# The first attention unit of a gated-linear-attention and expert-MLP kernel, written out by itself with 64x64 score tiles

## The chip, the cores and the metric

The kernel runs on one core of one Trainium2 chip. The metric is the device time of one execution in microseconds (us); the time of a kernel is the median of its runs. PE (TensorE) multiplies, DVE (VectorE) and ACT (ScalarE) do elementwise work, POOL (GpSimd) clears and copies, SP (SyncE) issues loads. PSUM is where products arrive; the other tiles lie in SBUF.

## The reference

The output of a gated recurrent attention is the input of four expert networks, whose outputs are summed with normalised weights. Setup and the bridge between the two are cut.

```python
# q, k, v, alpha: (4, 8, 768, 48)
for t in range(S):
    state = alpha[:, :, t, :, None] * state + np.einsum('bhd,bhe->bhde', k[:, :, t], v[:, :, t])
    y[:, :, t] = np.einsum('bhd,bhde->bhe', q[:, :, t], state)
# x = y as (3072, 384); domain_probs (3072, 4); w1 (4, 384, 1024); w2 (4, 1024, 384)
p = domain_probs / (domain_probs.sum(-1, keepdims=True) + 1e-09)
for e in range(E):
    h = np.maximum(x @ w1[e], 0.0)
    out += p[:, e:e + 1] * (h @ w2[e])
```

## The kernel before

The sequence is cut into blocks of 128 steps. A *unit* is one block of one batch entry with all eight heads: 6 blocks x 4 entries = 24 units. The eight heads are laid out as four pairs of two, each head padded from 48 to 64 rows, so that the transposed alpha, K and Q (`AT`, `KT`, `QT`) are tiles of 128 partitions x 4 pairs x 128 steps.

Inside a unit the products of decays are built by levels. At level `li` (m = 1, 2, 4, ... 64) the steps fall into groups of 2m; each query in the later half of a group meets the keys in the earlier half. `copy_q` (L317) copies the queries of the later halves into a cleared block tile `qb`, one copy for each head of a pair, so that one full-height matmul gives both heads. `next_q` (L324) then multiplies those queries of QT, in place, by the decay of the level; `dec` (L326) makes the next, coarser decay; `next_k` (L337) multiplies the earlier keys into the next of a ring of KT tiles, and a copy (L336, on GpSimd for unit 0, on ScalarE for all others) carries the other keys over. `products` (L344) computes the scores of a level, eight matmuls of 128x64 tiles with 64 columns. `take` (L354) places them by mask into `near`, a tile of 64-key halves; the term of a step with itself is a product, a sum over 48 and a multiplication with an identity (L287, L288, L370). Level 6 (`far`, L399) pairs the two halves of the block. Evictions and copies (L412, L417) make the triangular score tile `lat`; `result` (L439) multiplies it with V and evicts 128 columns of x (L452). Where a block follows, `turn_keys` (L460) and `sps` (L474) put the unit's keys and values into the state, copied by L482.

The expert network is tiled in groups of up to four units (512 columns of x). `up` computes the hidden layer (L547 for the first group), `down` the second product (L648). Group 0 has two units. Its slot 0 is worked by itself, so that the network starts as soon as unit 0 is done; unit 1 and the rest of unit 0 are threaded in between the steps of slot 0 by a queue of (due time, generator) pairs that `advance` serves. The pieces of the weights are later split into parts on ScalarE and VectorE and written back to memory (L222 to L229); that starts with the second slot.

The order on every engine is the order in which the program was written out; engines wait for each other by semaphores. SP issues, in order: alpha, K, Q and V of unit 0 (L173), the same of unit 1, the domain probabilities `p_all` (L769), four pieces of w1 (L209), then alpha, K and Q of unit 2, and four pieces of w2 (L213). Unit 0 is written out at the start with a hand-written interleaving of unit 0, unit 1 and zero products (`fill`, L780), which keep PE busy while the other engines work:

```python
        fill(7)
        for u, n in ((0, 2), (0, 3), (0, 4), (0, 5), (0, 5), (0, 4), (0, 3), (1, 0), (0, 0), (0, 2),
                     (0, 2), (1, 2), (0, 2), (1, 0), (0, 0), (0, 4), (0, 4), (0, 0)):
            next(runs[u])
            fill(n)
        norm_probs()
```

`norm_probs` (L253 to L257) normalises the domain probabilities, five small instructions on VectorE.

Of the kernel before, what the change touches and what calls it, by code (L numbers as in the profile page):

```python
# [10 lines left out]
F32 = mybir.dt.float32  # L11
F32R = mybir.dt.float32r
U32 = mybir.dt.uint32
U8 = mybir.dt.uint8
# [6 lines left out]
def kernel(  # L21
# [37 lines left out]
    nc = tc.nc  # L59

    B, H, S, D = q.shape
    E, DM, F = moe_w1.shape
    P = 128
    NCB = S // P
    NP = H // 2
    HD = 64
    QUAD = 32
    VD = D + QUAD
    KC = DM // P
    FCH = F // P  # L70
    NT = B * P
    NQ = 4
    QF = F // NQ
    FPQ = FCH // NQ
    LEVELS = [1 << i for i in range(7)]
    HALF = P // 2
# [2 lines left out]
    FINE = 1 + 1 / 4096  # L79
    TRIM = 1 - 1 / 8192  # L80

    PAD = 32

    j = np.arange(P)[:, None] % HALF
    n = np.arange(QUAD)[None, :]
    mask_np = np.stack([(j // (2 * m) == n // m) & (j % (2 * m) < m) for m in LEVELS[:6]],
                       1).astype(np.uint8)
    ident_np = np.concatenate([np.eye(P), np.tile(np.eye(HALF), (2, 1))], 1).astype(np.float32)

    const = ctx.enter_context(tc.tile_pool(name="const", bufs=1))  # L90
    wts = ctx.enter_context(tc.tile_pool(name="wts", bufs=2))
    dram = ctx.enter_context(tc.tile_pool(name="dram", bufs=1, space=bass.MemoryType.DRAM))
    work = ctx.enter_context(tc.tile_pool(name="work", bufs=2))
    hid = ctx.enter_context(tc.tile_pool(name="hid", bufs=2))
    ps = ctx.enter_context(tc.tile_pool(name="ps", bufs=2, space=bass.MemoryType.PSUM))

    ident_all = const.tile([P, P + HALF], F32, name="ident")
    ident = ident_all[:, :P]
    masks = const.tile([P, 6, QUAD], U8, name="masks")
    NBLK = B * NCB  # L100
    p_all = const.tile([P, NBLK, E], F32, name="p_all")
    tot = const.tile([P, NBLK], F32, name="tot")
# [2 lines left out]
    near = const.tile([P, H, HALF], F32, name="near")  # L105
    lat = const.tile([P, H, P], F32, name="lat")
# [7 lines left out]
    half = B // 2  # L114
# [18 lines left out]
    def raw(u, nm):  # L133
        return values[u % 2] if nm == "v" else apart[nm] if u == 1 else early[nm]

    xTs = {}
# [30 lines left out]
    def load(u, names):  # L167
        if u >= len(units):
            return
        cb, b = units[u]  # L170
        for nm in names:
            src = srcs[nm][b, :, cb * P:(cb + 1) * P, :].rearrange("h s d -> s h d")
            nc.sync.dma_start(out=raw(u, nm)[:, :, :D], in_=src)  # L173
# [7 lines left out]
    AHEAD = 4  # L181
# [70 lines left out]
    def norm_probs():  # L252
        nc.vector.reduce_sum(out=tot, in_=p_all, axis=AX.X)  # L253
        nc.vector.tensor_scalar_add(out=tot, in0=tot, scalar1=1e-9)
        nc.vector.reciprocal(out=tot, in_=tot)
        nc.vector.tensor_mul(p_all, p_all, tot.unsqueeze(2).broadcast_to([P, NBLK, E]))
        nc.vector.tensor_scalar_mul(out=p_fine, in0=p_all, scalar1=FINE)  # L257


    def halves(t, m):  # L260
        return t.rearrange("p a (b two r) -> p a b two r", two=2, r=m)

    def turned(src):
        tp = ps.tile([P, NP, P], F32, name="tp", tag="w")
        for p in range(NP):
            nc.tensor.transpose(tp[:, p, :], src(p), ident)  # L266
        return tp

    def attention(u):
        cb, b = units[u]  # L270
        ra, rk, rq, rv = (raw(u, nm) for nm in ("a", "k", "q", "v"))
# [3 lines left out]
        AT = work.tile([P, NP, P], F32, name="AT")  # L275
        QT = work.tile([P, NP, P], F32, name="QT")
        nc.scalar.copy(out=AT, in_=turned(pair(ra)))
        after = u + 2 if u == 0 else u + 1 if u > 1 else len(units)
        load(after, "a")
        yield  # L280
        KT = keys()
# [7 lines left out]
            load(after, "k")  # L289


        alone = u == 0
        if not alone:
            own_terms()
        yield
        nc.vector.tensor_mul(QT, turned(pair(rq)), AT)
        if alone:
            own_terms()
        load(after, "q")
        yield  # L300
# [19 lines left out]
        def next_q(li):  # L320
            m = LEVELS[li]
            qv = halves(QT, m)[:, :, :, 1, :]
            dv = halved(decs[li])
            nc.vector.tensor_mul(qv, qv, spread(dv[:, :, :, 0], m))  # L324
            dec = work.tile([P, NP, P // (2 * m)], F32, name=f"dec{li}", bufs=1 + 8 * (li == 6))
            nc.vector.tensor_mul(dec, dv[:, :, :, 0], dv[:, :, :, 1])  # L326
            decs.append(dec)

        def next_k(li):
            m = LEVELS[li]  # L330
            old = new = halves(KTs[li], m)
            if li + 1 < len(LEVELS):
                KTs.append(keys())
                new = halves(KTs[-1], m)
                copy = nc.gpsimd.tensor_copy if alone else nc.scalar.copy
                copy(out=new[:, :, :, 1, :], in_=old[:, :, :, 1, :])  # L336
            nc.vector.tensor_mul(new[:, :, :, 0, :], old[:, :, :, 0, :],  # L337
                                 spread(halved(decs[li])[:, :, :, 1], m))

# [49 lines left out]
        next_k(5)  # L389
        yield  # L390
        copy_q(6)
        next_q(6)
        yield
        bank = scores()
        far = ps.tile([P, NP // 2, 2, HALF], F32, name="far", tag="sc")
# [17 lines left out]
        yield  # L413
        for s in range(2):
            rows = slice(HALF * s, HALF * (s + 1))
            copy = nc.vector.tensor_copy if alone and s else nc.scalar.copy
            copy(out=lat[rows, :, rows], in_=near[rows])  # L417
        KT = KTs[-1]
        yield

# [272 lines left out]
    def cost(layer, gi, e):  # L693
        n = len(groups[gi]) / 4
        if layer == 0:
            return 2.1 * n if split1(gi, e) else 2.6 * n
        return 4.1 if gi > 1 else 4.7 if split2(gi, e) else 5.4
# [50 lines left out]
    def advance(spent):  # L748
        nonlocal clock
        clock += spent  # L750
        while waiting and clock >= waiting[0][0]:
            next(waiting.popleft()[2], None)

    with tc.manual_schedule():
        nc.scalar.dma_start(out=ident_all, in_=nc.inline_tensor(ident_np, name="ident_c").ap())
        nc.scalar.dma_start(out=masks, in_=nc.inline_tensor(mask_np, name="masks_c").ap())
        nc.gpsimd.memset(sts[B - 1], 0.0)
        for nm in "akq":
            for r in (early[nm], apart[nm]):
                nc.gpsimd.memset(r[:, :, D:], 0.0)  # L760
        nc.gpsimd.memset(lat[HALF:, :, :HALF], 0.0)
        for t in values + blocks:
            nc.gpsimd.memset(t, 0.0)
        for t in sts[:-1]:
            nc.gpsimd.memset(t, 0.0)

        load(0, "akqv")
        load(1, "akqv")
        nc.sync.dma_start(out=p_all, in_=moe_domain_probs.rearrange("(n p) e -> p n e", p=P))  # L769
        for i in range(NQ):  # L770
            load_piece(0, i)

        idle = ps.tile([P, P], F32, name="idle", tag="g", bufs=4)
        zeros = sts[B - 1].rearrange("p a i d -> p (a i d)")[:, :P]

        def fill(n):
            for _ in range(n):
                nc.tensor.matmul(idle, lhsT=zeros, rhs=zeros, start=True, stop=True)  # L780

        runs = [attention(u) for u in range(len(groups[0]))]
        fill(7)
        for u, n in ((0, 2), (0, 3), (0, 4), (0, 5), (0, 5), (0, 4), (0, 3), (1, 0), (0, 0), (0, 2),
                     (0, 2), (1, 2), (0, 2), (1, 0), (0, 0), (0, 4), (0, 4), (0, 0)):
            next(runs[u])
            fill(n)
        norm_probs()

        span = cost(0, 0, 0) * FCH / 2 + cost(1, 0, 0)  # L790
        waiting.extend((span * (k + 1) / 15, u, runs[u])
                       for k, u in enumerate([1, 1, 1, 0, 1, 0, *[1] * 8]))
        for fc in range(FCH):
            up(0, 0, fc, slice(0, 1))
            advance(cost(0, 0, 0) / 2)
        down(0, 0, [0], deque())
        while waiting:
            next(waiting.popleft()[2], None)
        clock = 0.0
        waiting.extend((1.0 + k, 1, runs[1]) for k in range(2))  # L800
        waiting.extend(deal())

        for (gi, e), after in zip(tasks, [*tasks[1:], (None, None)]):
            rest = gi == e == 0
            for fc in range(FCH):
                up(gi, e, fc, slice(1, len(groups[0])) if rest else None)
                advance(cost(0, gi, e) / (2 if rest else 1))
            each = len(groups[gi]) if split2(gi, e) else 1
            turns = [range(k, k + each) for k in range(rest, len(groups[gi]), each)]
            for k, slots in enumerate(turns):  # L810

                between = deque()
                if after[1] == 0:

                    for step, at in enumerate((0.0, 0.3, 0.42, 0.54) if gi == 0 else
                                              (0.0, 0.6, 0.7, 0.78)):
                        at = at * len(turns) - k
                        if 0 <= at < 1:
                            between.append((at, lambda step=step: split_x(after[0], step)))
                down(gi, e, slots, between)  # L820
        while stores:
            stores.popleft()()
# [28 lines left out]
```

## Time and profile before

| what | value |
|---|---|
| median of 3 runs | 1051.72 us (1050.86 to 1052.37) |
| the profiled execution | 1051.34 us, its span 1049.6 us |
| PE, DVE, ACT busy | 1032.5, 778.2, 565.6 us |
| unit 0's Q product starts (L296) | 7.95 us |
| its last take starts (L354) | 20.78 us, two of them, 0.91 us |
| first product of the network (L547) | 24.39 us |
| unit 1's result on PE (L439) | 42.04 us |
| second slot of the first expert starts (L547) | 44.45 us |

Times in the views are us from the start of the span. In a timeline a line gives start, length, engine, line of the program, operation, output and inputs, shapes (partitions x elements), how many were merged, and in brackets the idle time before it with what ended it. A matmul on 32-bit data appears as two records, so `x64` of the score products is 32 matmuls; a transpose is one record. The chain of waits lists, in order of time, the piece of work that each next one waited for.

### The profile page before, as it was taken

Reading aid. Unit: us, or ns where it says so; the run is one execution under the profiler, and the core shown is the slowest. Engines: PE = TensorE matmul, PEld = TensorE weight load, DVE = VectorE, ACT = ScalarE, POOL = GpSimd, SP = SyncE. Lnnn points to the kernel's source line nnn. Section 1 sums busy time; section 2 is a strip of 40 time slices with the busy share of each in tenths; the row PEclk is TensorE's granted clock in tenths of the full one; section 3 lists DMA queues with packets and bytes.
Section 4 is the critical chain, followed back from the end, with each engine's and each line's share of the span. In section 5 each row is a group of like instructions: output and inputs, shape, how many; then the busy total and the mean of one; then the engine's idle time right before and its main releaser. Section 6 shows DMA issues by size and latency. Waiting matters only on the chain.

```text
span 1049.6 us, 21621 instructions
## 1 busy us (share of the span) xinstructions
PE 1032.5 (98%) x8554; PEld 898.8 (86%) x8554; DVE 778.2 (74%) x1620; ACT 565.6 (54%) x1195; POOL 37.9 (4%) x81
## 2 busy tenths in 40 slices
PE   8899999999999999999999999999999999999998
PEld 8777777687787899898898998898988989898998
DVE  5578787668879868778877777977887875656565
ACT  4787877585666546446446436565464453323232
POOL 3000010000001000000000000000000000000000
PEclk9999999999999999999999999999999999999999
DMA  9397789887868948768669559577595454444531
GB/s 208 92 327 253 220 302 366 305 337 240 285 241 278 384 153 300 288 194 301 255 214 338 184 209 376 185 257 277 162 352 196 166 211 180 181 186 175 209 153 46
DMA packets 145493, 251.65 MB, mean 240 GB/s; under 512 B 107089, under 2 KB 121809, under 8 KB 122865
## 3 DMA queue, kind: packets, MB, share of 16 engines
q1 hardware_dynamic: 138928, 207.88, 57.9%
q0 software_dynamic: 6016, 42.08, 10.1%
q8 instruction: 67, 1.10, 0.4%
q10 hardware_dynamic: 448, 0.32, 0.1%
q14 instruction: 34, 0.27, 0.1%
HBM read 207.79 MB, written 42.47 MB: 238 GB/s over the span
## 4 chain that ended last, share of the span: by engine, by line
PE 86%; DVE 5%; ACT 5%; DMA 2%; issue 2%; POOL 0%; SPq 0%; ACTq 0%; DVEq 0%; POOLq 0%
PE ops L648 35%; PE one L555 23%; PE two L555 11%; PE sc L344 6%; PE yps L439 3%; PE tp L266 3%; PE one L547 2%; ACT qb L317 2%; PE sps L474 1%; PE far L399 1%; DMA w<-kept 1%; DVE near L354 1%; DMA rq<-in_q_dram 1%; PE idle L780 1%; DVE hT L601 1%
## 5 line engine op out<-in xcount | busy, mean ns | idle before, releaser
L648 PE MATMUL ops<-w,hT 128*128 128x384 f32 x1872 | 342.7, 339 | 0.2 <-DVE hT L601 0.2
L648 PEld LDWEIGHTS ops<-w,hT 128*128 128x128 f32 x1872 | 322.6, 188 | 4.0 <-ACT t L566 0.6
L555 PE MATMUL one<-xT,w 128*128 128x512 f32 x960 | 251.8, 398 | 0.8 <-DMA w<-kept 0.4
L555 PEld LDWEIGHTS one<-xT,w 128*128 128x128 f32 x960 | 176.1, 188 | 38.8 <-ACT t L566 1.2
L566 ACT ACTIVATE t<-one 128x512 f32<-128x512 f32 (+1 forms) x192 | 106.7, 556 | 175.8 <-PE one L555 170.2
L317 ACT COPY qb<-QT 64x256 f32<-64x256 f32 x336 | 136.7, 407 | 59.0 <-DVE QT L324 30.6
L595 DVE SCALAR_TENSOR_TENSOR hT<-t,hT 128x512 fp32r<-128x512 f32 (+1 forms) x172 | 110.3, 641 | 63.3 <-ACT hT L593 62.0
L568 DVE TENSOR_TENSOR t<-t,two 128x512 f32<-128x512 f32 (+1 forms) x172 | 109.2, 635 | 53.5 <-PE two L555 31.7
L593 ACT ACTIVATE hT<-t 128x512 fp32r<-128x512 f32 (+1 forms) x172 | 101.8, 592 | 86.8 <-DVE t L568 86.2
L555 PE MATMUL two<-xT,w 128*128 128x512 f32 x480 | 136.5, 393 | 0.1
L555 PEld LDWEIGHTS two<-xT,w 128*128 128x128 f32 x480 | 90.0, 188 | 20.5 <-DVE acc L677 0.9
L648 PE MATMUL ops<-hT 128*128 128x384 f32 x288 | 100.6, 491 | 0.3 <-DVE acc L677 0.3
L601 DVE SCALAR_TENSOR_TENSOR hT<-hT 128x512 fp32r<-128x512 f32 (+1 forms) x172 | 100.6, 633 | 0.0
L354 DVE COPY_PREDICATED near<-masks,sc 128x256 f32<-128x256 uint8 x144 | 77.0, 535 | 22.2 <-PE sc L344 19.2
L324 DVE TENSOR_TENSOR QT<-QT,dec 128x256 f32<-128x256 f32 x144 | 61.0, 423 | 38.9 <-ACT qb L317 38.4
L344 PEld LDWEIGHTS sc<-qb,KT 128*64 128x64 f32 x2304 | 72.7, 138 | 9.0 <-issue 4.8
L344 PE MATMUL sc<-qb,KT 128*64 128x64 f32 x2304 | 77.2, 223 | 2.6 <-ACT qb L317 2.6
L648 PEld LDWEIGHTS ops<-hT 128*128 128x128 f32 x288 | 52.1, 190 | 29.9 <-DVE acc L677 0.6
L677 DVE SCALAR_TENSOR_TENSOR acc<-ops,p_all,acc 128x384 f32<-128x384 f32 x82 | 49.7, 614 | 27.2 <-PE ops L648 26.3
L336 ACT COPY KT<-KT 128x256 f32<-128x256 f32 x138 | 57.5, 417 | 5.1 <-PE sc L344 1.9
L337 DVE TENSOR_TENSOR KT<-KT,dec 128x256 f32<-128x256 f32 x144 | 60.1, 417 | 0.0
L547 PE MATMUL one<-xT,w 128*128 128x256 f32 (+1 forms) x240 | 46.2, 340 | 0.6 <-ACT xT L452 0.6
(90 smaller groups left out, 954.4 us busy)
## 6 DMA issues: line engine op xcount, KB each, us to landing
w<-kept SPq DMA_DIRECT2D x144, 1152.0 KB, 8.2
kept<-w POOLq DMA_DIRECT2D x32, 1152.0 KB, 6.7
hT<-in_moe_w_dram SPq DMA_DIRECT2D x32, 384.0 KB, 6.1
w<-in_moe_w_dram SPq DMA_DIRECT2D x16, 384.0 KB, 6.1
rv<-in_v_dram SPq DMA_DIRECT2D x24, 192.0 KB, 7.3
ra<-in_alpha_dram SPq DMA_DIRECT2D x23, 192.0 KB, 6.1
rk<-in_k_dram SPq DMA_DIRECT2D x23, 192.0 KB, 5.8
rq<-in_q_dram SPq DMA_DIRECT2D x23, 192.0 KB, 5.8
```

The lines of the kernel that those rows point to most:

```text
L317: nc.scalar.copy(out=qb[rows, :, i, :].rearrange("p a (b r) -> p a b r", r=m), in_=qv[rows])
L324: nc.vector.tensor_mul(qv, qv, spread(dv[:, :, :, 0], m))
L344: nc.tensor.matmul(out[HALF * s:HALF * (s + 1), 2 * p:2 * p + 2, :], lhsT=KTs[li][:, p, HALF * s:HALF * (s + 1)], rhs=qbs[li][:, p, :, QUA ...
L354: nc.vector.copy_predicated(near.rearrange("p a (b two r) -> p a b two r", two=2, r=m)[:, :, :, 1, :], mk.unsqueeze(1).broadcast_to([P, H, ...
L547: nc.tensor.matmul(one, lhsT=w[:, kc], rhs=xraws[gi][:, kc, lo:hi], start=(kc == 0), stop=(kc == KC - 1))
L555: nc.tensor.matmul(out, lhsT=w[:, part, kc], rhs=x_part(gi, part, kc), start=(part == terms[0] and kc == 0), stop=(part == terms[-1] and k ...
L566: nc.scalar.activation(out=t, in_=one, func=ACT.Copy, scale=FINE)
L568: nc.vector.tensor_add(t, t, two)
L593: nc.scalar.activation(out=top, in_=x, func=ACT.Relu, scale=TRIM)
L595: nc.vector.scalar_tensor_tensor(out=low, in0=x, scalar=0.0, in1=top.bitcast(F32), op0=ALU.max, op1=ALU.subtract)
L601: nc.vector.scalar_tensor_tensor(out=dif, in0=top.bitcast(F32), scalar=1 / 4096.0, in1=low.bitcast(F32), op0=ALU.mult, op1=ALU.subtract)
L648: nc.tensor.matmul(sums[at], lhsT=h, rhs=w, start=(n == begins[at]), stop=(n == ends[at]))
```

## The change

Unit 0 gets a function of its own, `first_unit`, and its state update another, `rest_of_first`. The rest of the program is as before, apart from what the diff shows.

- There is a Q and a K tile for each level (`QTs`, `KTs`), in the buffers of the split weights `w1`, which are not in use yet. `next_q` and `next_k` (VectorE) write one half of the next tile, `same_q` and `same_k` (ScalarE) copy the other. Nothing is updated in place and no `qb` copies are made for this unit.
- Scores are products of 64x64 tiles: one matmul for each pair, head and half of the keys, 16 a level with 32 columns. The two heads of a pair go to two PSUM tiles, so `take` is two instructions of 128x128 a level.
- Own terms: Q before its decay (`plain`, from a second transposition of Q) times K in 16 matmuls of 64 columns, taken by an identity mask that is appended to the masks.
- The result is made in two halves of 64 steps, `y0` from `diag` alone and `y1` from `later_half`.
- Zero products behind the first seven: three of 128 columns and two of 384.
- SP's order: Q of unit 0 ahead of K; `p_all` behind the loads of w1 and of unit 2; `norm_probs` half-way through the hidden layer of slot 0.
- `next_q(6)` is left out in units of the first block, where there is no state; unit 1 computes its own terms after its Q product. Padding of one buffer shrinks (`PAD`).

```diff
+    mask_np = np.concatenate([mask_np.reshape(P, -1), j == np.arange(HALF)[None, :]], 1).astype(np.uint8)
...
+    def first_unit(fill, other):
...
+        AT = work.tile([P, NP, P], F32, name="AT")
+        QTs = [work.tile([P, NP, P], F32, name="QT")] + [next(place_of) for _ in range(6)]
+        KTs = [next(place_of) for _ in range(7)]
+        plain = next(place_of)
+        diag, later_half = (next(place_of).rearrange("p a (i n) -> p (a i) n", i=2) for _ in range(2))
+        nc.gpsimd.memset(diag, 0.0)
...
+        def same_q(li):
+            old, new = (used(t, li) for t in QTs[li:li + 2])
+            nc.scalar.copy(out=new[:, :, :, 0, :], in_=old[:, :, :, 0, :])
+
+        def next_q(li):
+            old, new = (used(t, li) for t in QTs[li:li + 2])
+            dv = halved(decs[li])[:, :, 1 if li == 5 else 0:, 0]
+            nc.vector.tensor_mul(new[:, :, :, 1, :], old[:, :, :, 1, :], spread(dv, LEVELS[li]))
...
+        def scored(outs, K, Q):
+            for p in range(NP):
+                for i in range(2):
+                    for s in range(2):
+                        rhs = Q(p, i, s)
+                        to = outs[i][keys[s], p]
...
+                        nc.tensor.matmul(to, lhsT=K[rows[i], p, keys[s]], rhs=rhs, start=True, stop=True)
...
+        nc.scalar.copy(out=AT, in_=turned(pair(ra)))
+        fill(1)
+        tq = turned(pair(rq))
+        dec(0)
+        nc.vector.tensor_mul(QTs[0], tq, AT)
+        same_q(0)
+        next_q(0)
+        tk = turned(pair(rk))
+        nc.scalar.copy(out=KTs[0], in_=tk)
+        same_q(1)
+        same_k(0)
+        dec(1)
+        dec(2)
+        next_q(1)
+        next_k(0)
+        fill(1, DM)
+        fill(1)
+        first = two("sc", HALF, tag="sc")
+        products(0, part(first, 0))
+        tq = turned(pair(rq))
...
+        load(2, "akq")
+        products(3, part(second, QUAD))
+        take(0, part(first, 0))
+        same_q(5)
+        next_q(5)
+        scored(part(second, HALF, HALF), KTs[0], lambda p, i, s: plain[rows[i], p, keys[s]])
...
+        fill(1, DM)
+        third = two("sc", HALF, tag="sc")
+        products(4, part(third, 0))
+        far = ps.tile([P, NP, HALF], F32, name="far0", tag="g", bufs=4)
+        for p in range(NP):
+            for i in range(2):
+                nc.tensor.matmul(far[rows[i], p], lhsT=KTs[6][rows[i], p, keys[0]],
+                                 rhs=QTs[6][rows[i], p, keys[1]], start=True, stop=True)
+        products(5, part(third, QUAD))
+        for i in range(2):
+            nc.scalar.copy(out=later_half[:HALF, NP * i:NP * (i + 1)], in_=far[rows[i]])
+        take(2, part(second, 0))
+        take(3, part(second, QUAD))
+        take(-1, part(second, HALF, HALF))
+        next(other)
+        take(4, part(third, 0))
+        take(5, part(third, QUAD))
+        for half, copy in ((0, nc.vector.tensor_copy), (1, nc.scalar.copy)):
+            of = slice(NP * half, NP * (half + 1))
+            copy(out=later_half[HALF:, of], in_=diag[HALF:, of])
+        fill(1)
+        next(other)
...
+        for s, (past, scores) in enumerate(((keys[0], diag), (slice(0, P), later_half))):
+            y = ps.tile([P, KC, HALF], F32, name=f"y{s}", tag="g", bufs=4)
+            for n, turn in enumerate(zip(*terms)):
+                for j, (c, h, at) in enumerate(turn):
+                    nc.tensor.matmul(y[QUAD * j:QUAD * (j + 1), c], lhsT=flat_v[past, at:at + QUAD],
+                                     rhs=scores[past, h], start=n == 0, stop=n == len(terms[0]) - 1)
+            nc.scalar.copy(out=xraws[0][:, :, HALF * s:HALF * (s + 1)], in_=y)
+        next_k(6)
+        return rest_of_first(AT, KTs[6], rv)
...
-        next_q(6)
+        if cb > 0:
+            next_q(6)
...
-        load(0, "akqv")
+        load(0, "aqkv")
         load(1, "akqv")
-        nc.sync.dma_start(out=p_all, in_=moe_domain_probs.rearrange("(n p) e -> p n e", p=P))
...
-        runs = [attention(u) for u in range(len(groups[0]))]
+        runs = [None, attention(1)]
         fill(7)
...
-        norm_probs()
+        runs[0] = first_unit(fill, runs[1])
+        nc.sync.dma_start(out=p_all, in_=moe_domain_probs.rearrange("(n p) e -> p n e", p=P))
...
             up(0, 0, fc, slice(0, 1))
+            if fc == FCH // 2:
+                norm_probs()
```

## The prediction

> **What bounds the kernel now.** I read the page first: is there one bound, or does the stage that changes have its own?
>
> ```profile
> span 1049.6 us, 21621 instructions
> PE 1032.5 (98%) x8554; PEld 898.8 (86%) x8554; DVE 778.2 (74%) x1620; ACT 565.6 (54%) x1195; POOL 37.9 (4%) x81
> ```
>
> PE fills the span, but the page's busy PE includes the zero products (L780) of the opening. The routed work cannot start before unit 0 has given its 128 columns of x, at 24.39 us. So I read the chain of waits of 7 to 25 us in order of time: what sets 24.39?
>
> ```profile
> 7.95 0.06 DVE QT L296
> ...
> 9.70 0.38 DVE QT L324
> ...
> 10.15 0.43 ACT qb L317
> ...
> 10.60 0.43 ACT qb L317
> ...
> 11.05 0.53 DVE QT L324
> ...
> 20.74 2.00 PE idle L780 x16
> 22.74 1.10 PE yps L439 x32
> ```
>
> The reader is to see a ping-pong: ScalarE copies the odd half of QT (two copies, 0.87), VectorE then multiplies it in place, then the next copy can start. VectorE's own timeline gives prices and both ends of the unit:
>
> ```profile
> 7.95 0.69 DVE L296 TENSOR_TENSOR QT<-tp,AT 128x512 f32<-128x512 f32 x1 [7.95 <-PE tp L266]
> 9.64 0.42 DVE L324 TENSOR_TENSOR QT<-QT,AT 128x256 f32<-128x256 f32 x1
> 11.05 0.51 DVE L324 TENSOR_TENSOR QT<-QT,dec 128x256 f32<-128x256 f32 x1 [0.32 <-ACT qb L317]
> 14.90 1.48 DVE L354 COPY_PREDICATED near<-masks,sc 128x256 f32<-128x256 uint8 x2
> 20.78 0.91 DVE L354 COPY_PREDICATED near<-masks,sc 128x256 f32<-128x256 uint8 x2
> 32.11 0.72 DVE L482 COPY st<-sps 64x192 f32<-64x192 f32 x2 [0.77 <-PE sps L474]
> ```
>
> From the Q product (7.95) to the end of the last take (21.69) VectorE is nearly gapless, 13.7 us. The last lines I need are of SyncE's timeline and of the landings:
>
> ```profile
> 8.51 1.10 SPq L769 DMA_DIRECT2D p_all<-in_moe_domain_probs_dram  x1
> rk<-in_k_dram SPq DMA_DIRECT2D x1, 192.0 KB, 4.3
> ```
>
> The second load of the queue lands 4.3 after its issue at 1.25, so at 5.55; the third at 1.87 + 4.9 = 6.8.
>
> **The change, part by part.** Intervals are start to start: a 128x256 product takes 0.42 but the next starts 0.34 later, a 128x128 one 0.20, a dependent one its full time plus 0.03.
>
> *Start.* Q becomes the second load, so its four transposes can run from 5.6 (spacing 0.213 there) and end at 6.6; the Q product runs 6.62 to 7.31 instead of 7.95 to 8.64: 1.3 us gained. K, third, lands at 6.8 and is copied by 8.2, ahead of its use.
>
> *VectorE from 7.34.* Each level has its own Q and K tile, so products no longer wait for copies. Six next_q (five at 0.34, the last of half size 0.20): 1.90. Six next_k: 2.04. Five dec (0.28, 0.22, 0.18, 0.16, 0.15 long, three dependent): 0.94. Takes are two per level of 128x128 instead of one of 128x256. At run lengths 1 and 2 one 128x256 took 0.74, i.e. about twice 256 element-times plus 0.17; for half the size I get 0.44, 0.36 to the next: 4 x 0.36 = 1.44. At the other four levels 0.45 becomes 0.31, interval 0.23: 8 x 0.23 = 1.84. Own terms by mask, two of 128x256 at 0.36: 0.72; the old product, reduction and near (0.55 + 0.55 + 0.68) go. Sum 8.88, so the last take ends at 7.34 + 8.88 + 0.08 = 16.3. Unit 1's 0.68 + 0.55 + 0.55, which stood ahead of the last takes, now stands behind them, and so does next_k(6).
>
> *ScalarE* over the same stretch: twelve tile copies at interval 0.33 (row L336), four evictions at 0.47 (L277) and two of far at 0.37 (L412), about 6.6 of 9 us. It hides under VectorE; without cover it would only add where next_q waits for same_q, and the copies run ahead of their users. POOL loses six copies and gains one memset at its end, about 7.2 us, needed at 11.
>
> *PE.* A product level is 16 matmuls of 64x64 tiles with 32 columns, 32 records. The trace shows no tile of 64 rows. Its single records show column tiles starting 0.007 apart and the same tile again 0.058 later for 64 columns (sc), 0.108 for 128 (yps). If row tiles run side by side likewise, four records take at most 0.058: 0.46 a level. If they do not, pairs of 0.058: 0.93. Worst, a tile is held for the whole 0.138 that a 64-column weight load is recorded with: 1.10. I take 0.46, nearest to yps, where four tiles do start together. Then PE has from 6.9: five transposes 2.2, zero products 1.8, six levels 2.8, own terms 0.46, far 0.46, y 0.93, together 8.6 of 10.5 us: covered by VectorE.
>
> *Tail.* Before: last take 21.69 to first L547 24.39 is 2.70, of which zero products held PE until 22.72. After: half of y needs no copy and starts at the last take; the copies end near 16.8, the second half of y takes 0.46 + 0.17, its eviction 0.36, waits 0.1: the first product of the network at 17.9. That is 6.5 before 24.39.
>
> *What takes some back.* norm_probs (22.50 to 23.84, 1.34 in the shadow of yps) moves into unit 1's levels. The 0.77 that VectorE idled before L482 absorbs part; 0.57 stays, queued ahead of near, the state copies and next_q(3). next_q(6) of the first units falls away (0.34 + 0.15 each); VectorE waits for qb there, so I count nothing.
>
> *Loads.* p_all leaves its place ahead of the weights, so these issue 1.1 earlier. Even as before, the first piece lands at 9.65 + 7.0 = 16.65 against 17.9, the last at 20.1 against about 22.4: hidden. p_all now lies behind Q of unit 2: by that load's 22.8 and its own packets (16 bytes each, 1.9 us before) at 23.5 to 24.7, and norm_probs comes at about 24: 0 to 0.7. The second weights land at 27.2 and are needed at 34.71 - 6 = 28.7: the cover is 1.5.
>
> *Sum.* -6.5 + 0.6 = -5.9 with nothing unforeseen; with no row tiles side by side, PE carries 11.9 instead of 8.6 and the start comes at 19.5: -4.3; with 1.10 a level, at 21.4: -2.4. Every form switch of PE that I can see costs about 0.1 (sc to idle 0.151 against 0.058) and there are eleven; some will reach the path, and p_all may too. I take -5.2. Behind 24.39 the order is as before and no queue is tied to the clock on the wall (DMA is nearly idle from 27 to 30), so the shift lasts to the end. The profiled execution took 1051.34 (span 1049.6 and 1.7 around it), 0.4 under the median 1051.72: 1046.1, and 1046.4 beside the median.
>
> *Rules of the Trainium skill.* TensorEngine Tiling (Array Packing), Key Properties, speaks against the change: changing the tiling mode drains TensorE. The row beside it is the 0.151 just named. If each of the eleven switches stood on the path, that rule would make -5.9 into about -4.8, an estimate; by the rows, with VectorE last, none does. TensorE: Matmul & The Clock Gate, Part 1, says that about 3.4 us of idling halves the clock. The trace shows the spacing go from 0.213 to 0.110 at 6.2 us after 5.0 gapless, and no fall after the 1.3 idle before L399; by that rule my longest gap, 0.6, would cost nothing.
>
> **The rivals.**
> 1. *PE becomes the bound* (row tiles one after another). For: no row of 64 rows; 32 records a level where there were 16. Against: the 0.007. Time: -2.4 to -4.3, 1047.4 to 1049.3.
> 2. *The gain is given back.* The second weights or p_all come late once all moves up by 6. For: DMA is busy without a break until 26. Against: the margins above. Each us past them costs one: 1048 to 1051.5.
> 3. *Slower: TensorE stays at, or falls back to, half clock* because 42 zero products behind the first seven became two wide and three narrow ones. For: the spacing was 0.213 until 6.2 though the page's clock row shows full clock throughout (so spacing is the measure), and small tiles leave the array half empty. Against: no gap over 0.6. At half rate 8.6 of PE work becomes 17: 6.9 + 17 + 0.4 = 24.3, the gain is gone, and 0.6 for norm_probs stays. Each further 3.4 us at half rate costs up to 1.7, so it decides from 5 us past the network's start; until 40 us: +3 to +5, about 1055.
>
> **How the numbers follow.** Forecast 0.62, PE bound 0.20, given back 0.10, half clock 0.08. What a measurement can tell from no change is about 0.2%, 2.1 us: 1049.6 to 1053.8. Faster: 0.62 + 0.19 + 0.04 = 0.85. Same: 0.01 + 0.06 + 0.01 = 0.08. Slower: 0.07, all half clock. Range: below, -6.5 with no loss, 1044.8; above, all of the PE bound and half of the given back, 1050.0; what is left out is mostly the half clock.
>
> **What would show it.** Q product near 6.6; VectorE gapless to a last take near 16.3; a product level of about 0.46; the first product of the network near 18; unit 1's state copies 0.6 later relative to it. Wrong if takes wait for PE (rival 1), if the spacing of full-width records returns to 0.21 (rival 3), or if the first products of the network wait for weights.

## The result and the profile after

The changed kernel takes 1049.24 us, the median of 15 runs (1047.68 to 1050.75); the kernel before took 1051.4 beside it. The ratio is 0.9979, 95% interval 0.9971 to 0.9987: faster by about 2.2 us, where 5.2 was forecast. The profiled execution took 1048.3, 3.0 under that of before. The network's first product moved from 24.39 to 21.71 instead of to 17.9. A profile shows one execution, and executions of a kernel differ: the mean granted clock was 0.996 to 0.998 in 14 of the 15 runs and 1.0 in one (1048.03), and in experiment 1 0.998 in three of seven (1047.89 to 1049.48, the profiled one) and 0.999 to 1.0 in four (1046.38 to 1047.45).

The page's first part says that little work changed:

```profile
span 1046.5 us, 21812 instructions
PE 1028.6 (98%) x8652; PEld 892.9 (85%) x8652; DVE 775.4 (74%) x1617; ACT 564.5 (54%) x1195; POOL 35.7 (3%) x76
```

PE has 98 records more, and its busy time fell by 4 us. So I went to PE's timeline of the opening. The columns are start and duration in us, engine, line, output from inputs, tile, shapes and count; the bracket gives the idle time before the group and what ended it.

```profile
9.43 0.67 PE L326 MATMUL sc<-w,w 64*64 64x32 f32 x32
9.92 0.65 PE L326 MATMUL near<-w,w 64*64 64x32 f32 x32
...
13.34 0.71 PE L326 MATMUL sc<-w,w 64*64 64x32 f32 x16 [0.25 <-ACT w L311]
15.14 0.64 PE L326 MATMUL sc<-w,w 64*64 64x32 f32 x14 [1.09 <-issue]
...
17.43 1.12 PE L268 MATMUL tp<-ident,hT 128*128 128x128 f32 x4
...
18.66 0.60 PE L268 MATMUL tp<-ident,hT 128*128 128x128 f32 x4
19.20 1.11 PE L437 MATMUL y<-w,rv 64*32 64x64 f32 x52
20.87 0.42 PE L437 MATMUL y<-w,rv 128*32 128x64 f32 x12 [0.57 <-issue]
21.71 0.49 PE L732 MATMUL one<-xT,w 128*128 128x128 f32 x2 [0.42 <-ACT xT L439]
```

Three things are to be seen. The levels are as cheap as forecast: 9.43 to 9.92 is 0.49 for one. Level 4 stops in its middle, after 16 of 32 records, for 1.09 us, and y stops after 52 of 64 for 0.57; both gaps end at "issue", which means that PE waited for nothing that the profile knows of. And behind the first gap the same transposes take 1.12 that take 0.60 a little later. VectorE's timeline shows what that does to the takes:

```profile
6.32 0.69 DVE L354 TENSOR_TENSOR QT<-tp,AT 128x512 f32<-128x512 f32 x1
...
14.43 0.76 DVE L337 COPY_PREDICATED w<-masks,near 128x256 f32<-128x256 uint8 x2
17.43 0.89 DVE L342 COPY_PREDICATED w<-masks,sc 128x128 f32<-128x128 uint8 x4 [2.24 <-PE sc L326]
```

VectorE is done with everything else at 15.19, as its ledger had it, and then stands for 2.24 us for PE. The table of stretches, cut at the borders of the granted clock, has PE's busy time and count first and the granted clock (PEclk) third from the end:

```profile
11.73:15.14 3.41, 2.06 (x54) 1.23 (x47) 3.06 (x12) 1.56 (x6) 0.00 (x0) 1.00 1.08 340
15.14:18.55 3.41, 3.41 (x69) 3.34 (x69) 1.14 (x6) 0.73 (x2) 0.00 (x0) 0.50 1.14 208
25.38:28.79 3.41, 2.14 (x20) 1.95 (x18) 2.68 (x10) 3.33 (x12) 0.00 (x0) 1.00 0.52 194
```

TensorE ran at half clock for one stretch of 3.41 us, beginning just where the gap ended. The page's row of tenths shows only nines there: the slices are 26 us wide. Before, the clock was full from 6.2 us to the end of the span.

The chain of waits, which before ran over the zero products of 20.74, now runs over the gaps (start, duration, what):

```profile
14.04 1.09 issue
...
20.30 0.57 issue
...
21.71 1.62 PE one L732 x12
```

**Where the gaps come from.** I counted PE's instructions in the trace. A 32-bit matmul is two records, each with its weight load, so four instructions; a level of eight matmuls had 32 of them, one of sixteen has 64. The gaps stand at instruction 449 and 705, 256 apart. The page's part on the queues has one that moves instructions in packets of 16 KB (68 of them, 1.11 MB), which would be 64 bytes for each of 256:

```profile
q8 instruction: 68, 1.11, 0.4%
```

I read this as blocks of 256 with borders at 193, 449 and 705: in every kernel run here one packet began as PE came to 193 or after that, the next as it came to 449 or after that, and between the Q product and the network PE stood at "issue" nowhere but ahead of 449 and 705. So the packet that belongs to one border is taken to bring the block beyond the next. After that packet had ended, a block that PE was waiting for was begun 1.17 to 1.65 us later (thirteen gaps in eight kernels). In us, from the times of the packets and of PE's instructions in the trace:

| kernel | passes 193 | packet | 449: wanted, begun | packet | 705: wanted, begun |
|---|---|---|---|---|---|
| before | 13.18 | 13.15–14.62 | 21.56, no gap | 21.68–22.85 | 33.45, no gap |
| changed | 9.78 | 12.65–13.72 | 14.05, 15.14 | 17.81–19.26 | 20.30, 20.87 |

The kernel before used the 256 instructions up to 449 in 8.4 us; the changed kernel gets through them in 4.3, and they are not there in time. That is theory 1: PE's supply of instructions holds it up, and the idle time brings a stretch at half clock. Rivals: the waits belong to the products (a tile, a copy), the half clock comes by itself, or the zero products and the second transposition of q cost the time.

### The profile page after: what moved, and what is told of

It reads as the page before. It is cut to its first block, busy times and chain, and to the rows that moved or that the text cites. A ratio compares the mean times of both kernels' runs of the same rounds, so it can differ in the third digit from the quotient of the medians.

```text
span 1046.5 us, 21812 instructions
## 1 busy us (share of the span) xinstructions
PE 1028.6 (98%) x8652; PEld 892.9 (85%) x8652; DVE 775.4 (74%) x1617; ACT 564.5 (54%) x1195; POOL 35.7 (3%) x76
## 3 DMA queue, kind: packets, MB, share of 16 engines
q8 instruction: 68, 1.11, 0.4%
## 4 chain that ended last, share of the span: by engine, by line
PE 88%; DVE 6%; ACT 4%; issue 2%; DMA 0%; SPq 0%; ACTq 0%; DVEq 0%
PE ops L833 36%; PE one L740 23%; PE two L740 11%; PE sc L529 6%; PE yps L624 3%; PE tp L268 3%; PE one L732 2%; ACT qb L503 1%; PE sps L659 1%; PE far L585 1%; DVE hT L786 1%; DVE near L539 1%; DVE QT L510 1%; DVE acc L862 1%; DMA rk<-in_k_dram 0%
## 5 line engine op out<-in xcount | busy, mean ns | idle before, releaser
L503 ACT COPY qb<-QT 64x256 f32<-64x256 f32 x322 | 130.9, 406 | 53.8 <-DVE QT L510 30.0
L740 PEld LDWEIGHTS two<-xT,w 128*128 128x128 f32 x480 | 90.0, 188 | 20.5 <-DVE acc L862 0.9
L539 DVE COPY_PREDICATED near<-masks,sc 128x256 f32<-128x256 uint8 x138 | 73.8, 535 | 23.8 <-PE sc L529 21.1
L510 DVE TENSOR_TENSOR QT<-QT,dec 128x256 f32<-128x256 f32 x135 | 56.8, 421 | 35.5 <-ACT qb L503 35.0
L529 PEld LDWEIGHTS sc<-qb,KT 128*64 128x64 f32 x2208 | 69.6, 138 | 8.9 <-issue 4.7
L529 PE MATMUL sc<-qb,KT 128*64 128x64 f32 x2208 | 74.0, 223 | 2.6 <-ACT qb L503 2.6
L522 DVE TENSOR_TENSOR KT<-KT,dec 128x256 f32<-128x256 f32 x138 | 57.6, 417 | 0.0
```

The costliest lines, as they stand in the source:

```text
L503: nc.scalar.copy(out=qb[rows, :, i, :].rearrange("p a (b r) -> p a b r", r=m), in_=qv[rows])
L529: nc.tensor.matmul(out[HALF * s:HALF * (s + 1), 2 * p:2 * p + 2, :], lhsT=KTs[li][:, p, HALF * s:HALF * (s + 1)], rhs=qbs[li][:, p, :, QUA ...
L539: nc.vector.copy_predicated(near.rearrange("p a (b two r) -> p a b two r", two=2, r=m)[:, :, :, 1, :], mk.unsqueeze(1).broadcast_to([P, H, ...
L740: nc.tensor.matmul(out, lhsT=w[:, part, kc], rhs=x_part(gi, part, kc), start=(part == terms[0] and kc == 0), stop=(part == terms[-1] and k ...
```

## The experiments

All edits are to the changed kernel. Times and ratios are against the kernel before, run beside them.

**1. One result instead of two.** 32 matmuls for y become 16, so 705 lies beyond the network's start.

```diff
-        for s, (past, scores) in enumerate(((keys[0], diag), (slice(0, P), later_half))):
...
+        nc.vector.tensor_copy(out=lat[:HALF, :, :HALF], in_=diag[:HALF])
+        nc.scalar.copy(out=lat[HALF:, :, HALF:], in_=diag[HALF:])
...
+        y = ps.tile([P, KC, P], F32, name="y", tag="w")
+        for n, turn in enumerate(zip(*terms)):
...
+                                 rhs=lat[:, h], start=n == 0, stop=n == len(terms[0]) - 1)
```

> The changed kernel, with the result of unit 0 made once for all 128 steps (16 matmuls of 128 columns, as every other unit does it) instead of twice for 64 steps. Theory 1, PE gets its instructions in blocks of 256 and the next block is late: the changed kernel's two stalls stand at PE instructions 449 and 705, 256 apart. Here y ends at instruction 662, so 705 falls some 21 matmul records into the first layer, about 23.5 us, when that block has long come (20.9): the gap of 0.57 in y is gone and no other takes its place; the first product of the network at about 21.5 instead of 21.71 (one pass of y costs 0.9 behind the copies instead of 0.45, which eats most of the gain). Theory 2, the stalls are waits for data that the profile does not show: the gap belongs to y, stays about 0.6, and the network starts at 22.0 to 22.3. Whole time: theory 1 -0.2 us against the changed kernel, theory 2 +0.4.

Measured: 1047.45, ratio 0.9965 (0.9954 to 0.9977). Three lines of PE's timeline of this kernel:

```profile
15.11 0.55 PE L326 MATMUL sc<-w,w 64*64 64x32 f32 x13 [1.12 <-issue]
...
19.84 1.08 PE L435 MATMUL y<-lat,rv 128*32 128x128 f32 x32 [0.59 <-ACT lat L418]
21.52 2.72 PE L730 MATMUL one<-xT,w 128*128 128x128 f32 x22 [0.60 <-ACT xT L437]
```

The gap in y is gone and the one in level 4 stays, as theory 1 has it. The network starts only 0.19 earlier: y now waits for both copies (0.59 ahead of it, ended by ScalarE's `lat`). The profiled execution took 1049.48, so its timeline does not explain the lower median.

**2. Loads later.** Only alpha, K and Q of unit 1 are issued first; the rest follows behind the second transposition of q.

```diff
-        load(1, "akqv")
-        for i in range(NQ):
-            load_piece(0, i)
+        load(1, "akq")
...
         tq = turned(pair(rq))
+        load(2, "q")
+        for i in range(NQ):
+            load_piece(0, i)
+        load(1, "v")
```

> The changed kernel with another order of SyncE's loads: Q of unit 2, which has to wait until PE has read Q of unit 0 for the second time (about 9.4 us), now stands ahead of the four pieces of w1, and V of unit 1 behind them; so the DMA queues run empty at about 10.5 us. Theory 1 (late instruction blocks, held up behind loads in the DMA queues): the first 16 KB instruction fetch, which ran at 12.65 in the changed kernel though instruction 193 was passed at 9.8, runs at about 10.7; no stall at instruction 449, no half clock behind it, takes of levels 4 and 5 at about 15.3 instead of 17.43. The second fetch is then asked for at about 14.0 among the w1 pieces and comes at 18.5 to 19.5, so the gap in y grows to 1.5 to 2.5 us; first product of the network at 19.7 to 20.5 instead of 21.71; whole time -1.2 to -2.0 against the changed kernel. Theory 2 (waits for data): the gap of 1.09 stays where it is, and with w1 later the network starts at 21.7 to 22.7.

Measured: 1050.02, ratio 0.9987 (0.9978 to 0.9996). PE's timeline:

```profile
21.54 0.64 PE L441 MATMUL y<-w,rv 128*32 128x64 f32 x12 [3.58 <-issue]
22.60 1.65 PE L736 MATMUL one<-xT,w 128*128 128x128 f32 x6 [0.42 <-ACT xT L443]
```

The first packet came at 11.11 to 12.07 instead of 12.65 to 13.72, the gap in level 4 disappeared, and the takes of the last levels began at 15.65. But I had expected the network at 19.7 to 20.5: the second packet came at 19.07 to 20.24, PE reached instruction 705 at 17.96, and the gap grew from 0.57 to 3.58, with 6.8 us at half clock (20.37 to 27.19). What one block gave, the next took.

**3. Zero products left out,** all five `fill` calls of the opening behind the first seven.

> The changed kernel without the five zero products that stand behind the first seven (they are no part of the result). If the zero products hold the clock (theory A): without them TensorE falls to half clock in two or more stretches of 3.4 us between 7 and 25 us instead of one, full-width records 0.213 apart, and the first product of the network comes 1 to 2 us later than 21.71. If the one half-clock stretch came only from the stall of 1.09 us (theory B): one stretch again, and the network starts within 0.3 us of 21.71. By the theory of late instruction blocks, the 21 PE instructions fewer move the stalls 21 instructions further on in the program, still at instructions 449 and 705.

Measured: 1050.39, ratio 0.9993 (0.9984 to 1.0002), no difference that these runs show. PE's timeline:

```profile
13.30 0.82 PE L326 MATMUL sc<-w,w 64*64 64x32 f32 x24 [1.09 <-ACT w L311]
15.29 0.32 PE L326 MATMUL sc<-w,w 64*64 64x32 f32 x8 [1.16 <-issue]
```

Eight records fewer in front put the gap behind 24 records instead of 16. Half clock lasted from 16.25 to 26.49, three stretches of 3.41. The network began at 21.77, hardly later, but its first 30 records took 5.85 us instead of 3.62. The ratio is 0.9993 here and 0.9979 with them; the intervals overlap a little, so by the whole time it is likely, not shown, that the zero products earn their place.

**4. Own terms on VectorE,** as in the kernel before: no second transposition of q, no product for the own terms, and multiplication, sum and diagonal on VectorE instead of the masked copy.

```diff
-        tq = turned(pair(rq))
-        nc.scalar.copy(out=plain, in_=tq)
...
-        take(-1, part(second, HALF, HALF))
+        nc.vector.tensor_mul(own, rq[:, :, :D], rk[:, :, :D])
+        nc.vector.reduce_sum(out=dot, in_=own, axis=AX.X)
+        nc.vector.tensor_mul(diag.rearrange("p (i a) n -> p i a n", i=2),
```

> The changed kernel with unit 0's own terms made as before: product, sum and multiplication with the identity on VectorE (1.78 us) instead of 16 matmuls, a second transposition of Q and two masked copies (0.72 us). Theory 1 (instruction blocks of 256): 72 PE instructions fewer, so instruction 449 is the fifth record of level 5 instead of the 17th of level 4; level 4 and far run at once, the takes of level 4 start at 15.5 to 16 instead of 17.43, the stall waits for the block at about 15.1 in level 5, and instruction 705 falls into the network's first products: no gap in y. The network starts at 19.5 to 20.5; whole time -1.2 to -2.2 against the changed kernel. Theory 2 (the gap belongs to level 4's second half, and VectorE is the bound): the gap stays in level 4, VectorE's extra 1.06 us falls into its idle 2.24, no gain: 21.5 to 22.5.

Measured: 1050.46, ratio 0.9989 (0.9978 to 1.0). PE's timeline:

```profile
14.99 0.88 PE L325 MATMUL sc<-w,w 64*64 64x32 f32 x30 [2.54 <-ACT w L310]
```

Neither border has a gap, but the network began at 21.28 and not at the expected 19.5 to 20.5: the 1.78 us on VectorE (11.38 to 13.24) stood ahead of takes 0 and 1, whose PSUM tiles level 4 needs. The bracket names ScalarE's copy, which ended as level 4 began; but PE's own semaphore instructions, at 14.89 and 15.17, wait for VectorE and come 0.04 behind the two halves of take 1 (ended at 14.85 and 15.13). A wait of 2.54 took the gap's place and half clock followed (15.91 to 19.32). The run mixes two causes and says little about the own terms by themselves.

**5 and 6. Edits 1 and 2 together, then fewer instructions still.** In the second, the first seven zero products become two of 384 columns and one of 128, sixteen PE instructions fewer.

```diff
-        fill(7)
+        fill(2, DM)
+        fill(1)
```

> The changed kernel with both edits: one result for 128 steps, and Q of unit 2 ahead of the w1 loads. Theory 1 (instruction blocks of 256, held up behind loads): no stall at instruction 449 (the loads' order gave the first fetch at 11.1), and instruction 705 lies 21 matmul records into the network's first products. The first product starts at 18.7 to 19.7 instead of 21.71; instruction 705 is reached 2.3 us later, at 21 to 22, while the second block came at 21.5 in the run with that order of loads: a stall of 0 to 0.5 there. No stretch at half clock before the network. Whole time 2 to 3.5 us under the changed kernel, 1 to 2 under the one with one result alone. Theory 2 (the stalls move with the work around them): a stall of 1 to 3 us shows up elsewhere before the network, which starts at 21 or later.

> As the kernel with both edits, and the first seven zero products of 128 columns replaced by two of 384 and one of 128 (the same time, 16 PE instructions fewer; no part of the result). Theory 1: instruction 705 falls another 8 matmul records, 0.9 us, further into the network, so what is left of the stall there goes; otherwise the same times within 0.3 us in the first unit; whole time 0 to 0.5 us under the kernel with both edits. Theory 2: no difference, or a stall that stays at the same product.

Measured: 1045.78, ratio 0.9948 (0.9935 to 0.996), and 1046.11, ratio 0.9953 (0.9941 to 0.9966). PE's timeline of the first:

```profile
14.66 0.38 PE L326 MATMUL sc<-w,w 64*64 64x32 f32 x13 [0.69 <-issue]
...
19.61 3.62 PE L734 MATMUL one<-xT,w 128*128 128x128 f32 x30 [0.60 <-ACT xT L441]
```

and of the second:

```profile
13.49 1.05 PE L326 MATMUL sc<-w,w 64*64 64x32 f32 x32 [0.25 <-ACT w L311]
...
19.05 3.62 PE L734 MATMUL one<-xT,w 128*128 128x128 f32 x30 [0.60 <-ACT xT L441]
```

Each edit by itself left one block late. Together they leave a gap of 0.69, where none was expected, and no half clock: the first packet came at 11.77 to 13.37 instead of at 11.1. In the second there is no gap. That is not shown to come of the sixteen instructions: PE reached 449 only 0.12 later (14.09 against 13.97), while the packet had ended 0.76 earlier (12.61), for which no cause was found. The network starts 0.56 earlier in the second; the two medians do not tell them apart.

**7 and 8. norm_probs out of unit 1's levels:** the load of the domain probabilities behind the pieces of w1, `norm_probs` right behind the first unit; once on top of 6, once on the changed kernel alone.

```diff
-            if fc == FCH // 2:
-                norm_probs()
...
         runs[0] = first_unit(fill, runs[1])
+        norm_probs()
```

> As the kernel before it in this call, and the domain probabilities loaded right behind the w1 pieces and normalised right behind unit 0 instead of half-way through slot 0. The forecast's term: the 1.34 us of VectorE that stood in unit 1's levels cost 0.57; in the changed kernel first product to second slot took 20.40 against 20.06 before, so 0.34. If that is their price, first product to second slot is 20.0 to 20.1 here and the whole time falls by 0.3 to 0.4. If the loads come so late that VectorE waits for p_all ahead of unit 1's levels, that stretch is longer than 20.4.

> The changed kernel with this one part undone: the domain probabilities loaded right behind the w1 pieces, ahead of unit 2's loads, and normalised right behind unit 0. First product to second slot 20.0 to 20.1 us instead of 20.40; the stalls at instructions 449 and 705 stay, since the DMA queues are as full as before (first 1.0 to 1.3, second 0.4 to 0.8 us); whole time 0.2 to 0.5 us under the changed kernel.

Measured: 1045.45, ratio 0.9947 (0.9933 to 0.996), and 1047.96, ratio 0.9974 (0.9963 to 0.9985). From the network's first product to the second slot it is 20.16 and 20.14, where 20.0 to 20.1 was expected and the changed kernel has 20.40. VectorE did wait for the domain probabilities in experiment 7, 1.40 us, and the stretch was not longer for it. In the second the gaps stayed, 0.96 and 0.24 (expected 1.0 to 1.3 and 0.4 to 0.8). Experiment 7 has the lowest median, though the runs do not tell it from 5 and 6; its timelines of PE, VectorE and ScalarE:

```profile
17.13 1.08 PE L440 MATMUL y<-lat,rv 128*32 128x128 f32 x32 [0.65 <-ACT lat L423]
18.81 3.62 PE L735 MATMUL one<-xT,w 128*128 128x128 f32 x30 [0.60 <-ACT xT L442]
```

```profile
14.46 0.76 DVE L337 COPY_PREDICATED w<-masks,near 128x256 f32<-128x256 uint8 x2
15.19 0.90 DVE L342 COPY_PREDICATED w<-masks,sc 128x128 f32<-128x128 uint8 x4
...
19.99 0.25 DVE L255 TENSOR_REDUCE tot<-p_all 128x24 f32<-128x96 f32 x1 [1.40 <-DMA p_all<-in_moe_domain_probs_dram]
```

```profile
15.86 0.58 ACT L471 COPY KT<-tp 128x512 f32<-128x512 f32 x1 [0.28 <-PE tp L268]
16.46 0.61 ACT L423 COPY lat<-w 64x512 f32<-64x512 f32 x1
18.28 0.48 ACT L442 COPY xT<-y 128x384 f32<-128x384 f32 x1 [1.20 <-PE y L440]
```

With PE supplied, the last takes stand right behind the own terms and end at 16.09.

**9. Four zero products more,** of 32 columns, behind the first seven, where PE waits for Q anyway. They do nothing but move the count.

```diff
         fill(7)
+        fill(4, 32)
```

> The changed kernel with four zero products of 32 columns more, right behind the first seven. They are computed with TensorE waiting for Q anyway, so they cost 0.2 us at most where they stand. What they change is the count: each is two records and four PE instructions (a weight load and a matmul for each record), so every later matmul comes eight records later in the count. Theory of the instruction blocks: the two gaps are not tied to a matmul but to the numbers 449 and 705 of PE's instructions, so each gap moves forward by eight records in the program, to behind 8 of level 4's 32 records (it was behind 16), and to behind 44 of y's 64 records (it was behind 52). Its end stays within 0.5 of 15.1, since the fetch does not move. Rival (the gap belongs to the products: a PSUM tile, a copy or a semaphore that level 4 waits for): it stays behind 16 records, or lies at a level's edge, and four products more move nothing.

PE's timeline:

```profile
13.78 0.59 PE L326 MATMUL sc<-w,w 64*64 64x32 f32 x8 [0.25 <-ACT w L311]
14.62 0.49 PE L326 MATMUL sc<-w,w 64*64 64x32 f32 x21 [0.26 <-issue]
...
17.29 1.00 PE L437 MATMUL y<-w,rv 64*32 64x64 f32 x44
19.67 0.53 PE L437 MATMUL y<-w,rv 128*32 128x64 f32 x20 [1.39 <-issue]
```

Both gaps moved by exactly the eight records: behind 8 of level 4, behind 44 of y. They belong to the count and not to any product: the rival of a tile, copy or semaphore is out. In this single run (1048.01, profiled) the first packet came 1.4 earlier than in the changed kernel, at 11.24, with the same loads; the gap was 0.26, and the clock stayed full. Why the packet came earlier is open.

**10. PE kept busy:** one zero product more ahead of level 4, the fetch untouched.

```diff
-        fill(1, DM)
+        fill(2, DM)
         third = two("sc", HALF, tag="sc")
```

> The changed kernel with one zero product more of 384 columns just ahead of level 4 (two records, 0.9 us), in the time in which TensorE was going to stand still. The fetch of the instructions is untouched, so level 4 is still held up until about 15.1, the gap only gets shorter, 0.5 to 0.7 instead of 1.09, and lies behind 14 of the 32 records. Theory of the clock: the half clock of 15.14 to 18.55 came from the time that TensorE stood still in the 3.4 us before (1.09 and 0.25); with 0.6 it does not come (the kernel with one result and later loads had 0.69 and 0.25 and kept the full clock). Then far, level 5 and the transposes run at full clock, the last takes start at 16.3 to 16.7 instead of 17.43, the first product of the network at 20.4 to 21.0 instead of 21.71, and the time is 0.7 to 1.3 under the changed kernel. Rival (the half clock comes from the small tiles of the levels, whatever the gap): the half clock comes as before, nothing gained, and 0.3 to 0.5 lost where the added product is late.

Measured: 1049.39, ratio 0.9984 (0.9974 to 0.9993). PE's timeline:

```profile
14.94 0.48 PE L326 MATMUL sc<-w,w 64*64 64x32 f32 x18 [0.65 <-issue]
...
20.85 0.42 PE L437 MATMUL y<-w,rv 128*32 128x64 f32 x14 [2.22 <-issue]
21.70 2.60 PE L732 MATMUL one<-xT,w 128*128 128x128 f32 x12 [0.43 <-ACT xT L439]
```

The theory of the clock held in this execution: gap 0.65, full clock until 22.09, and the takes began at 16.35 instead of 17.43. The expected time did not: instruction 705 was reached at 18.64 instead of 20.30, and its block was begun at 20.85, as in the changed kernel (20.87). So the half clock was not what set the changed kernel's network start: the second block was, which in these two kernels begins 0.84 and 0.85 before it. Here the long gap in y brought half clock behind it, 22.09 to 25.51, and took back what was left.

## Why the prediction was right and wrong

- **Start and VectorE.** Right. The Q product began at 6.32 (forecast 6.62). The last take was to end at 16.3; with PE supplied it ended at 16.09 (experiment 7). The takes, the products and the own terms cost what the rows before gave.
- **ScalarE, loads, clearing.** Right: in the changed kernel the longest wait for a load behind the Q product's start is 0.53 (PE, for K), the longest of VectorE for a ScalarE copy 0.34, and the network did not wait for weights.
- **PE.** The disputed price was right: 0.49 from one level to the next, 0.45 from its first record to its last (eight rounds of four tiles, most of them 0.058 apart), against bounds of 0.46 and 1.10. Rival 1 is out: row tiles run side by side. Its sign came all the same, takes that wait for PE (2.24), and was due to the late block. A switch of form costs the 0.1 forecast: level to transposes 0.60, level to level 0.49.
- **The step that failed: "8.6 of 10.5 us: covered by VectorE".** It counted what the matmuls take and not that their instructions have to arrive. The count of the levels doubled, the pace of the opening doubled too, and no row before showed what a late block costs, because there every block came ahead of its use. "My longest gap, 0.6" was wrong with it: 1.09, and the half clock behind. The network started 3.8 us after the forecast. The experiments that took the gaps away, with the result made once, brought 2.66 (experiment 6: 21.71 to 19.05) and 2.90 of it back (experiment 7: 18.81); the other 0.9 is the tail's. The Trainium skill, Runtime: NRT & Kernel Launch, Instruction fetch mechanics, knows the blocks of 256 instructions and says that crossing a border is mostly hidden; here it cost 0.24 to 3.58 where the pace was high. The same section gives PE room for 2048 instructions, and further on speaks of only two lines of 16 KiB; the packets here fit the two, since each block was fetched only after PE had entered the one before it.
- **Tail.** Forecast 1.6 from the last take's end to the network. Mis-sized: in experiment 7, with the result made once, it was 2.72 (16.09 to 18.81). The copies end 0.98 behind the last take (17.07) and not 0.5, since ScalarE first evicts unit 1's K (15.86, 0.58) and begins its copy at 16.46; the one pass of y behind them takes 1.08 where 0.46 + 0.17 was forecast for the second of two, and its eviction 0.48 instead of 0.36. In the changed kernel the tail was 3.39 (18.32 to 21.71), 0.57 of it the gap, and y's start at 19.20 stands behind transposes of unit 1.
- **norm_probs.** Forecast 0.57, measured 0.34 (first product to second slot 20.06 before, 20.40 after); taking it out gave 0.24 to 0.26 back.
- **To the end.** Right in the main: the shift was 2.33 at 45 us, still 2.31 at 160, and 3.04 at the end of the profiled execution. Of that growth 0.43 is a wait for `w<-kept` at 162.30 that the kernel before shows and the changed one does not. The direction was right too, while a gain like the forecast's 5.2 came only with experiments 5 to 7 (5.11, 4.78 and 1050.89 - 1045.45 = 5.44).
- **Rival 3** named the half clock with the wrong trigger and price. It came for one stretch, not for good, and behind the late block. The wide zero products did not bring it, since leaving all five out made it three stretches; and with the same five and the blocks in time it did not come (experiment 7). But their number does bear on it, as the rival had it: one more ahead of level 4 kept the full clock there (experiment 10).
- **The clock rule** that I weighed (the Trainium skill, TensorE: Matmul & The Clock Gate, Part 1: half clock after about 3.4 us of idling) did not fit. The stretch that brought half clock had PE busy for 2.06 of its 3.41 us.

## What to carry to other kernels

When a change cuts matmuls into more and smaller ones, count the engine's instructions as well as its time: what needs 256 of them in 4 us at the start of a kernel, beside a burst of loads, can run ahead of its own instruction stream. A gap in the middle of a uniform group that ends at "issue" and moves when unrelated instructions are added in front was such a border here, not a dependency. Take such gaps away together: here the cures of the first gap alone (experiments 2 and 10) handed their gain to the next block, the cure of the second alone (experiment 1) left the first, and only both at once made the gain stay.

## What the runs showed of the hardware

- **Instruction blocks.** PE passed border 193 and the packet for the block beyond the next began at once in the kernel before (13.18, 13.15), 2.9 us later in the changed kernel (9.78, 12.65), 0.9 later with loads issued later (10.17, 11.11). Waiting behind the loads' packets fits these three, but is not shown: experiment 9 had the changed kernel's loads and a delay of 1.1, and experiments 5 to 7 had the later loads and delays of 2.1, 1.1 and 1.0.
- **Clock.** The granted clock changed at borders a multiple of 3.41 us apart, and the busy time that halved it differed from stretch to stretch. Stretches with level 4 in them led to half clock at 1.78, 2.03, 2.06 and 2.20 us busy (experiments 3 and 1, the changed kernel, experiment 8), and to full clock at 2.47 and 2.76 (experiments 5 and 10). A stretch of experiment 9 with tiles of 128 rows alone kept it at 1.75, and the changed kernel's of 25.38 at 2.14:

```profile
18.42:21.84 3.42, 1.75 (x31) 1.59 (x31) 1.01 (x3) 0.57 (x2) 0.00 (x0) 1.00 0.88 85
```

So a 64x64 tile may count for less than one of 128 rows; no run varies this alone, so it is a guess. With very little work any stretch led to half clock: 0.81, 0.92 and 1.00 us busy (experiments 10, 4 and 2).
- **Tiles of 64 rows.** Four 64x64 tiles with 32 columns start 0.006 to 0.007 us apart and the same four again 0.058 later, as the column tiles of the kernel before do (0.007, and 0.058 with 64 columns).
